# Last batch of top-32 attention with a low-rank mixer: first heads and results turned by the vector engine

## The chip, the cores and the metric

The kernel runs on one core of a Trainium2 chip. The metric is device time in microseconds (us) for one execution of the whole program. In the profile PE is TensorE (PEld its weight loads), DVE VectorE, ACT ScalarE, POOL GpSimd, and SP the engine whose queue issues the transfers.

## The reference

For each of 8 batches and 8 heads, attention over 576 positions of 64 values keeps the 32 largest scores of each row. The result, heads side by side, goes through a low-rank mixing along the sequence and a two-layer block. All is float32.

```python
scores = scale * np.matmul(q, k.transpose(0, 1, 3, 2))
kth = np.partition(scores, -32, axis=-1)[..., -32:-31]
scores = np.where(scores >= kth, scores, -1e9)
attn = np.exp(scores - scores.max(-1, keepdims=True))
attn = attn / (attn.sum(-1, keepdims=True) + 1e-09)
x = heads_side_by_side(np.matmul(attn, v))         # (8, 576, 512)
u = x + (x.transpose(0, 2, 1) @ U @ V).transpose(0, 2, 1)   # rank 32
out = u + np.maximum(u @ w_ch1, 0.0) @ w_ch2       # 512 -> 2048 -> 512
```

## The kernel before

*Tiling.* Two heads make a pair g; 4 pairs make a batch, 32 pairs the whole (`NPAIR`, `NP`). The 576 rows of a pair go in five chunks t: four of 128 rows for each of the two heads, and t=4 with the last 64 rows of both heads side by side. So there are 160 steps n = 5 g + t (`CH` is 5).

*One step of the main loop.* It works on several chunks at once. `front(n)` finds the 32nd largest score on DVE: MAX8 `first` (L385), then three times MATCH_REPLACE8 (L395) and MAX8 `m` (L399), for each of two heads; in t=4 there is one such chain, not two. ACT and POOL then mask the row and take the exponential into E (L402, L403, L419 to L421, L351). `scores(n+1)` (L320, L333) are on PE, copied to Ssb by ACT (L344 to L346); the next `first` waits for them. `turns(n-1)` turns E with PE transposes into PT (L474 and a copy on ACT, L475; the last 64 columns L479, L480). `values(n-2)` multiplies PT with v into O (L508, L512; L498 for t=4). PE's order in a step is: turns of the chunk two steps back, values of it, scores of the next chunk, with the block's matmuls in between.

*Second heads.* From step 30 on (`ROUNDED`), the second head (h=1) of the chunks t<4 isn't turned on PE (`shared`). `blocks(n-1)`, called in the middle of step n, lets DVE transpose its 32x32 blocks into y (L446). Four transfers write y to a buffer `away` in DRAM (L452), and one brings it back into the second half of PT (L456).

*The two-layer block as filler.* When the four pairs of a batch are mixed (`mixed`, L533 to L566), `mlp(b)` is put into `fillers`. `fill()`, called eight times in a step, adds a credit and draws so many matmuls of the block (L581 up into hT, L600 down), which spreads the block of batch b over the attention of batch b+1. The last batch's block has nothing to lie beside and comes at the end. The hT tiles are a ring of `HT` = 10 tiles of two blocks of rows; a half of a block (`SPAN`) uses 8 of them.

*Results.* A finished tile oT (L615, L616) is laid in `late`; `turned_back` turns it some matmuls later with two or three PE transposes (L648) and copies on ACT (L650, L652), and stores it with one or two transfers (L654, L659). In the last batch, all but the last tile are turned by DVE (L630) and stored by 8 or 12 transfers (L635, L640).

*Order.* PE, ACT, DVE and POOL each run their instructions in the order in which the code emits them; only SP's queue is ordered by the framework.

Of the kernel before, what the change touches and what calls it, by code (L numbers as in the profile page):

```python
# [8 lines left out]
F32 = mybir.dt.float32  # L9
# [17 lines left out]
def kernel(  # L27
# [29 lines left out]
    B, H, S, D = q.shape  # L57
    P = 128
# [3 lines left out]
    NF, NC = F // P, C // P  # L62
    NT, TAIL = 4, 64
    MAIN = NT * P
    HALF = S // 2
    assert S == MAIN + TAIL and D == 64 and H % 2 == 0 and C == 512 and TOPK % 8 == 0
    NPAIR = H // 2
    NP = B * NPAIR

    CH = NT + 1  # L70
# [3 lines left out]
    NV = 3  # L74

    BLK = 32
    HT = 10
    PE, ACT = mybir.EngineType.PE, mybir.EngineType.Activation
    DVE, POOL = mybir.EngineType.DVE, mybir.EngineType.Pool

# [2 lines left out]
    attn = ctx.enter_context(tc.tile_pool(name="attn", bufs=2))  # L83
# [11 lines left out]
    SPAN = ((0, 2 * P + TAIL), (2 * P + TAIL, S))  # L95
# [30 lines left out]
    def rows(t):  # L126
        return P if t < NT else TAIL

    def cols(t):
        return slice(t * P, t * P + rows(t))  # L130
# [4 lines left out]
    def half(h):  # L135
        return slice(h * D, (h + 1) * D)
# [98 lines left out]
    probs, PTs = {}, {}  # L235
# [198 lines left out]
    def shared(g, t):  # L434


        return t < NT and g * CH + t >= ROUNDED

    def blocks(g, t):


        E2 = probs[g, t]
        PT = attn.tile([P, 2 * NT + 1, P], F32, tag="PT", name="PT")
        PTs[g, t] = PT
        y = attn.tile([P, 4, NT, BLK], F32, tag="y", name="y", bufs=1)
        nc.vector.transpose(  # L446
            y.rearrange("p r c j -> p c r j"),
            E2[:, S + TAIL : 2 * S].rearrange("p (c r j) -> p c r j", c=NT, r=4),
        )
        away = dram.tile([P, 4, P], F32, tag="away", name="away")  # L450
        for a in range(4):
            nc.sync.dma_start(  # L452
                away[:, a].rearrange("(r i) n -> i r n", r=4),
                y[a * BLK : (a + 1) * BLK].rearrange("i r c j -> i r (c j)"),
            )
        nc.sync.dma_start(  # L456
            PT[:, NT : 2 * NT].rearrange("p a n -> p (a n)"), away.rearrange("p a n -> p (a n)")
        )

    def turns(g, t):  # L460


        E2 = probs.pop((g, t))
        nh = 2 if t < NT else 1
        if shared(g, t):
            PT = PTs[g, t]
        else:
            PT = attn.tile([P, 2 * NT + 1, P], F32, tag="PT", name="PT")
            PTs[g, t] = PT
        for h in range(1 if shared(g, t) else nh):  # L470
            tp = ps_t.tile([P, NT, P], F32, tag="tp", name="tp")
            for j in range(NT):
                a = h * (S + TAIL) + j * P
                nc.tensor.transpose(tp[:, j, :], E2[:, a : a + P], ident)  # L474
            nc.scalar.copy(PT[:, NT * h : NT * h + NT], tp)  # L475
            yield
        tp = ps_t.tile([P, P], F32, tag="tp", name="tp")
        a = MAIN if nh == 2 else S - P
        nc.tensor.transpose(tp, E2[:, a : a + P], ident)  # L479
        nc.scalar.copy(PT[:, NT * nh], tp)  # L480
        yield

    def inverse(g, lo, hi):
        den = dens[g][:, lo:hi]
        if g == NPAIR - 1:
            nc.vector.tensor_scalar_add(den, den, 1e-9)
        nc.vector.reciprocal(den, den)

    def values(g, t):

        PT = PTs.pop((g, t))
        va, vd, vt = (a[g % NV] for a in (vas, vds, vts))
        O = ps_t.tile([P, P], F32, tag="tp", name="O")
        if t == NT:
            den, x = dens[g], xs[g % 2]
            inverse(g, 2 * NT if g == NPAIR - 1 else 0, 2 * NT + 1)
            for j in range(NT + 1):
                nc.tensor.matmul(  # L498
                    O,
                    lhsT=PT[:, j],  # L500
                    rhs=va[:, :, j, :] if j < NT else vt,
                    start=(j == 0),
                    stop=(j == NT),
                )
            for h in range(2):
                nc.scalar.mul(x[half(h), NT, half(h)], O[half(h), half(h)], den[half(h), 2 * NT :])
            return
        nc.tensor.matmul(O, lhsT=vd, rhs=PT[:, 2 * NT], start=True, stop=False)  # L508
        PB = PT[:, NT : 2 * NT].rearrange("p a (c j) -> p c a j", c=NT) if shared(g, t) else None
        for j in range(NT):  # L510
            for h in range(2):
                nc.tensor.matmul(  # L512
                    O[half(h)],
                    lhsT=va[:, h, j, :],
                    rhs=PB[:, j] if h and shared(g, t) else PT[:, NT * h + j],
                    start=False,
                    stop=(j == NT - 1),
                )
        if t == 0:
            XTs[g] = attn.tile([P, MAIN], F32, tag="XT", name="XT")  # L520
        nc.scalar.copy(XTs[g][:, cols(t)], O)  # L521
# [49 lines left out]
    def mlp(b):  # L571
# [3 lines left out]
        for chunks, (lo, hi) in zip(PARTS, SPAN):  # L575
            w = hi - lo
            hTs = []
            for f in range(NF):
# [11 lines left out]
                if f % 2 == 0:  # L590
                    hT = mlpp.tile([P, 2, WIDE], F32, tag="hT", name="hT", bufs=HT)
                    hTs += [hT[:, 0], hT[:, 1]]
# [28 lines left out]
    def turned_back(b, chunks, lo, c, oT):  # L621


        def run():
            cs = slice(c * P, (c + 1) * P)
            if b == B - 1 and (lo, c) != (SPAN[1][0], NC - 1):

                w = sum(rows(t) for t in chunks)
                ob = mlpp.tile([P, 3 * P], F32, tag="ob", name="ob", bufs=2)
                nc.vector.transpose(ob[:, 0:w], oT[:, 0:w])  # L630
                for a in range(4):
                    cs = slice(c * P + a * BLK, c * P + (a + 1) * BLK)
                    ba = ob[a * BLK : (a + 1) * BLK]
                    for t in chunks[0:2]:
                        nc.sync.dma_start(  # L635
                            out[b, 0:MAIN, cs].rearrange("(m i t) c -> t i m c", i=BLK, t=NT)[t],
                            ba[:, OFF[t] - lo : OFF[t] - lo + P].rearrange("i (m c) -> i m c", c=BLK),
                        )
                    if NT in chunks:
                        nc.sync.dma_start(  # L640
                            out[b, MAIN:S, cs].rearrange("(m i) c -> i m c", i=BLK),
                            ba[:, 2 * P : 2 * P + TAIL].rearrange("i (m c) -> i m c", c=BLK),
                        )
                return
            tp = ps_t.tile([P, 3, P], F32, tag="tp", name="tp")
            for i, t in enumerate(chunks):
                n = rows(t)
                nc.tensor.transpose(tp[0:n, i, :], oT[:, OFF[t] - lo : OFF[t] - lo + n], ident)  # L648
            ob = mlpp.tile([P, 3, P], F32, tag="ob", name="ob", bufs=2)
            nc.scalar.copy(ob[:, 0:2], tp[:, 0:2, :])  # L650
            if NT in chunks:
                nc.scalar.copy(ob[0:TAIL, 2], tp[0:TAIL, 2, :])  # L652
            t = chunks[0]
            nc.sync.dma_start(  # L654
                out[b, 0:MAIN, cs].rearrange("(p t) c -> p t c", t=NT)[:, t : t + 2, :],
                ob[:, 0:2],
            )
            if NT in chunks:
                nc.sync.dma_start(out[b, MAIN:S, cs], ob[0:TAIL, 2])  # L659

        return run
# [4 lines left out]
    STEPS = NP * CH  # L666
# [6 lines left out]
    def fill(k=1):  # L673


        nonlocal due
        for _ in range(k):
            if passes:
                passes.pop(0)()
            if mixing and next(mixing[0], True):  # L680
                mixing.pop(0)
            due += share * (SHORT if t == NT else 1) * (EARLY if n <= 2 * ALONE + 2 else 1)
            while due > 0:
                if not fillers:
                    due = 0.0
                    break
                done = next(fillers[0], None)
                if done is None:
                    fillers.pop(0)
                else:  # L690
                    due -= done
# [3 lines left out]
    t = 0  # L695
# [5 lines left out]
    for n in range(STEPS + 2):  # L701
        g, t = divmod(n, CH)
# [8 lines left out]
        if n >= ALONE - 1 and n <= ALONE:  # L711

            if n < ALONE:
                next(last)
                values(*divmod(n - 3, CH))
                list(turning)
                next(here)
                next(last)
                scores(*divmod(n + 1, CH))
                values(*divmod(n - 2, CH))  # L720
# [51 lines left out]
        away = n <= STEPS and shared(*divmod(n - 1, CH))  # L772
# [26 lines left out]
        if n <= STEPS:  # L799
            turning = turns(*divmod(n - 1, CH))  # L800
# [3 lines left out]
        if t in (1, 3):  # L804
            next_params(1)
        next(here, None)
        fill()
    while mixing or fillers:
        fill()
# [31 lines left out]
```

## Time and profile before

| | |
|---|---|
| time, median of 3 runs | 1774.49 us (1774.05 to 1775.44) |
| profiled execution, span | 1773.6 us |
| DVE transpose y, L446 | 104 x 0.69 us |
| transfers away<-y, L452 | 416 of 64 KB, 1.8 us to landing |
| transfers PT<-away, L456 | 104 of 256 KB, 2.8 us to landing |
| PE transposes of E, L474 | 736, listed with 0.283 us each |
| PT copy on ACT, L475 | 184 x 0.585 us |

A row of the groups gives line, engine, operation, `out<-in`, the number of instructions and their mean duration. Matmuls overlap one another, and their ends in the profile are modelled, so what one of them costs is read from the distance of the starts.

### The profile page before, as it was taken

The numbers are of one execution on the slowest core, as the hardware profiler recorded it, in microseconds if no ns is written. First come the engines' busy times: TensorE is split into PE (matmuls) and PEld (weight loads), VectorE is DVE, ScalarE is ACT, GpSimd is POOL, SyncE is SP. The second block draws the span as 40 slices with busy tenths as digits, with TensorE's granted clock in tenths as the row PEclk, the third lists the DMA queues.
The fourth block names the chain that finished last, engine by engine and source line by source line (L and its number), as shares of the span: only waits on it lengthen the run. The fifth ranks groups of instructions, "written<-read, shape, count | busy, mean of one in ns | idle before, by whom it ended". The sixth has DMA issues, their size and how long they took to land.

```text
span 1773.6 us, 28992 instructions
## 1 busy us (share of the span) xinstructions
PE 1669.3 (94%) x9851; PEld 1257.5 (71%) x9851; DVE 1560.3 (88%) x3106; ACT 1029.4 (58%) x2682; POOL 846.8 (48%) x591
## 2 busy tenths in 40 slices
PE   4666789999999999999999999999999999999999
PEld 2434556677777877788777877788777877788677
DVE  7999989899999999999999999999999999994000
ACT  4778777555656656565656656565656656564100
POOL 4777677535354554545445454444445444453000
PEclk7687799999999999999999999999999999999999
DMA  3222332222223332222233232232233232211010
GB/s 95 88 82 73 88 85 61 50 59 71 58 67 80 66 72 56 67 68 64 64 71 79 62 70 62 65 70 63 63 73 80 59 73 60 53 50 45 4 15 13
DMA packets 275829, 112.79 MB, mean 64 GB/s; under 512 B 173920, under 2 KB 260192, under 8 KB 275680
## 3 DMA queue, kind: packets, MB, share of 16 engines
q1 hardware_dynamic: 274624, 110.68, 26.4%
q8 instruction: 77, 1.26, 0.3%
q14 instruction: 72, 0.59, 0.1%
q10 hardware_dynamic: 1056, 0.26, 0.1%
HBM read 74.15 MB, written 36.70 MB: 63 GB/s over the span
## 4 chain that ended last, share of the span: by engine, by line
PE 75%; DVE 16%; POOL 4%; ACT 3%; issue 2%; DMA 1%; SPq 0%; POOLq 0%; DVEq 0%
PE mm L581 25%; PE mm L600 24%; DVE rr L395 7%; PE sc L333 6%; PE O L512 6%; DVE m L399 6%; PE tp L474 3%; DVE first L385 2%; PE sc L320 2%; PE O L498 2%; PE up L556 1%; PE O L508 1%; POOL E L402 1%; PE up L558 1%; PE tp L648 1%
## 5 line engine op out<-in xcount | busy, mean ns | idle before, releaser
L399 DVE MAX8 m<-rr 128x8 f32<-128x576 f32 x864 | 614.7, 748 | 5.5
L600 PE MATMUL mm<-hT,w 128*128 128x256 f32 (+1 forms) x2048 | 547.4, 410 | 0.0
L581 PE MATMUL mm<-uT,w 128*128 128x256 f32 (+1 forms) x2048 | 541.5, 410 | 0.9 <-ACT hT L593 0.9
L402 POOL TENSOR_SCALAR E<-Ssb,m 128x576 f32<-128x576 f32 x127 | 281.1, 2214 | 411.7 <-DVE m L399 409.1
L581 PEld LDWEIGHTS mm<-uT,w 128*128 128x128 f32 x2048 | 371.7, 190 | 115.1 <-issue 26.0
L600 PEld LDWEIGHTS mm<-hT,w 128*128 128x128 f32 x2048 | 368.3, 190 | 106.8 <-issue 22.5
L395 DVE MATCH_REPLACE8 rr<-m,rr 128x576 f32<-128x576 f32 x576 | 427.2, 742 | 0.0
L421 POOL TENSOR_TENSOR Ssb<-Ssb,E 128x576 f32<-128x576 f32 x159 | 225.4, 1418 | 122.3 <-ACT E L420 121.7
L351 ACT ACTIVATE E<-Ssb,nmax 128x576 f32<-128x576 f32 x288 | 223.3, 776 | 52.4 <-POOL Ssb L403 34.9
L593 ACT ACTIVATE hT<-mm 128x320 f32<-128x320 f32 (+1 forms) x256 | 105.1, 411 | 240.4 <-PE mm L581 240.1
L385 DVE MAX8 first<-Ssb 128x8 f32<-128x576 f32 x288 | 203.3, 742 | 31.4 <-ACT Ssb L346 31.4
L395 DVE MATCH_REPLACE8 rr<-first,Ssb 128x576 f32<-128x576 f32 x288 | 211.8, 742 | 0.0
L403 POOL TENSOR_TENSOR Ssb<-Ssb,E 128x576 f32<-128x576 f32 x127 | 179.3, 1412 | 10.6
L333 PE MATMUL sc<-qkT 64*128 64x288 f32 x1024 | 170.6, 454 | 6.7 <-ACT Ssb L344 5.8
L474 PE MATMUL tp<-ident,E 128*128 128x128 f32 x736 | 116.0, 283 | 37.1 <-ACT XT L521 14.6
L512 PE MATMUL O<-PT,va 128*64 128x128 f32 x2048 | 146.3, 284 | 1.9 <-DMA PT<-away 1.9
L474 PEld LDWEIGHTS tp<-ident,E 128*128 128x128 f32 x736 | 92.1, 145 | 68.7 <-ACT XT L521 16.6
L475 ACT COPY PT<-tp 128x512 f32<-128x512 f32 x184 | 106.6, 585 | 49.0 <-PE tp L474 46.4
L512 PEld LDWEIGHTS O<-PT,va 128*64 128x64 f32 x2048 | 113.7, 140 | 19.0 <-DMA PT<-away 2.9
L420 ACT ACTIVATE E<-Ssb,least 128x576 f32<-128x576 f32 x159 | 123.3, 776 | 5.2
L333 PEld LDWEIGHTS sc<-qkT 64*128 64x128 f32 x1024 | 93.3, 198 | 45.3 <-issue 14.3
L613 DVE TENSOR_TENSOR oT<-uT,mm 128x320 f32<-128x320 f32 (+1 forms) x8 | 3.6, 455 | 137.1 <-PE mm L600 137.1
(81 smaller groups left out, 1574.0 us busy)
## 6 DMA issues: line engine op xcount, KB each, us to landing
away<-y SPq DMA_DIRECT2D x416, 64.0 KB, 1.8
PT<-away SPq DMA_DIRECT2D x104, 256.0 KB, 2.8
raw<-in_moe_w_ch_dram SPq DMA_DIRECT2D x32, 512.0 KB, 3.8
va<-in_v_dram SPq DMA_DIRECT2D x64, 128.0 KB, 2.3
out_dram<-ob SPq DMA_DIRECT2D x57, 128.0 KB, 2.2
ld<-in_q_dram SPq DMA_DIRECT2D x108, 64.0 KB, 2.4
ld<-in_k_dram SPq DMA_DIRECT2D x108, 64.0 KB, 2.4
ld<-in_q_dram SPq DMA_DIRECT2D x108, 8.0 KB, 2.2
```

The costliest lines, as they stand in the source:

```text
L333: nc.tensor.matmul(sc[:, h, 0:HALF], lhsT=qkT[half(h), 0, cols(t)], rhs=qkT[half(h), 1, i * HALF : (i + 1) * HALF], start=True, stop=True,)
L351: nc.scalar.activation(E, chunk, AF.Exp, bias=nmax, scale=SCALE, accum_out=total)
L385: nc.vector.max(ms[c], curs[c])
L395: nc.vector.match_replace(nxt, ms[c], curs[c], NEG)
L399: nc.vector.max(ms[c], curs[c])
L402: nc.gpsimd.tensor_scalar(Es[c], chunks[c], ms[c][:, 7:8], NEG, ALU.is_lt, ALU.mult)
L403: nc.gpsimd.tensor_tensor(chunks[c], chunks[c], Es[c], ALU.add)
L421: nc.gpsimd.tensor_tensor(chunks[c], chunks[c], Es[c], ALU.subtract)
L474: nc.tensor.transpose(tp[:, j, :], E2[:, a : a + P], ident)
L512: nc.tensor.matmul(O[half(h)], lhsT=va[:, h, j, :], rhs=PB[:, j] if h and shared(g, t) else PT[:, NT * h + j], start=False, stop=(j == NT ...
L581: nc.tensor.matmul(ph[:, 0:w], lhsT=w1[:, cc, f * P : (f + 1) * P], rhs=uT[:, cc, lo:hi], start=(cc == 0), stop=(cc == NC - 1),)
L600: nc.tensor.matmul(po[:, 0:w], lhsT=w2[:, f, c * P : (c + 1) * P], rhs=hTs[f][:, 0:w], start=(f == 0), stop=(f == NF - 1),)
```

## The change

It concerns the last batch and the result of the batch in front of it.

- `both` names the chunks t<4 of the pairs 28, 29 and 30, the first three of the last batch. Their first heads, too, are turned by DVE and transfers: `blocks` gets the head h as an argument and is called a second time, for h=0, at the end of the step, after DVE's last MAX8 in it. `turns` leaves these heads out, and `values` reads both halves of PT in the order of the blocks.
- y gets two buffers instead of one, and HT goes from 10 to 9 to make room.
- The results of batch 6 are turned back as those of batch 7 are: DVE in place of PE and ACT, 8 or 12 transfers in place of 1 or 2.

It is meant to take work from TensorE where the profile shows it full.

```diff
-    HT = 10
+    HT = 9
...
+    def both(g, t):
+        return t < NT and (B - 1) * NPAIR <= g < NP - 1
+
-    def blocks(g, t):
+    def blocks(g, t, h=1):
         E2 = probs[g, t]
-        PT = attn.tile([P, 2 * NT + 1, P], F32, tag="PT", name="PT")
-        PTs[g, t] = PT
-        y = attn.tile([P, 4, NT, BLK], F32, tag="y", name="y", bufs=1)
+        if h:
+            PTs[g, t] = attn.tile([P, 2 * NT + 1, P], F32, tag="PT", name="PT")
+        PT = PTs[g, t]
+        y = attn.tile([P, 4, NT, BLK], F32, tag="y", name="y")
         nc.vector.transpose(
             y.rearrange("p r c j -> p c r j"),
-            E2[:, S + TAIL : 2 * S].rearrange("p (c r j) -> p c r j", c=NT, r=4),
+            E2[:, h * (S + TAIL) : h * (S + TAIL) + MAIN].rearrange("p (c r j) -> p c r j", c=NT, r=4),
         )
...
-            PT[:, NT : 2 * NT].rearrange("p a n -> p (a n)"), away.rearrange("p a n -> p (a n)")
+            PT[:, NT * h : NT * h + NT].rearrange("p a n -> p (a n)"), away.rearrange("p a n -> p (a n)")
...
-        for h in range(1 if shared(g, t) else nh):
+        for h in range(0 if both(g, t) else 1 if shared(g, t) else nh):
...
-            if b == B - 1 and (lo, c) != (SPAN[1][0], NC - 1):
+            if b >= B - 2 and (b, lo, c) != (B - 1, SPAN[1][0], NC - 1):
...
         next(here, None)
+        if n <= STEPS and both(*divmod(n - 1, CH)):
+            blocks(*divmod(n - 1, CH), 0)
         fill()
```

More of the change, by code (lines that the diff above doesn't have):

```diff
@@ L508, in values @@
         nc.tensor.matmul(O, lhsT=vd, rhs=PT[:, 2 * NT], start=True, stop=False)
-        PB = PT[:, NT : 2 * NT].rearrange("p a (c j) -> p c a j", c=NT) if shared(g, t) else None
+        swapped = both(g, t), shared(g, t)
         for j in range(NT):
@@ L514, in values @@
                     lhsT=va[:, h, j, :],
-                    rhs=PB[:, j] if h and shared(g, t) else PT[:, NT * h + j],
+                    rhs=(
+                        PT[:, NT * h : NT * h + NT].rearrange("p a (c j) -> p c a j", c=NT)[:, j]
+                        if swapped[h]
+                        else PT[:, NT * h + j]
+                    ),
                     start=False,
```

## The prediction

> **What bounds the kernel now.** I read the page first: the busy shares and the 40 slices.
>
> ```profile
> PE 1669.3 (94%) x9851; PEld 1257.5 (71%) x9851; DVE 1560.3 (88%) x3106; ACT 1029.4 (58%) x2682; POOL 846.8 (48%) x591
> PE   4666789999999999999999999999999999999999
> DVE  7999989899999999999999999999999999994000
> ```
>
> Both PE and DVE show nines to slice 36; the last 3.5 slices are PE alone, the second block's multiplication of the last batch. The change sits just ahead of that, so I cut the end of the run with the table by windows. Its edges are the first MAX8 of pairs 28, 29, 30 and 31 (the last batch), the end of DVE's last MAX8, and the first matmul of the last MLP. Columns: span, then busy PE, PEld, DVE, ACT, POOL.
>
> ```profile
> 1418.98:1469.76 50.78, 50.66 (x314) 39.42 (x313) 48.52 (x97) 29.96 (x81) 24.60 (x17) 1.00 0.32 74
> 1469.76:1519.37 49.61, 49.61 (x288) 35.43 (x287) 48.51 (x97) 30.41 (x81) 23.27 (x15) 1.00 0.26 60
> 1519.37:1569.28 49.91, 49.91 (x300) 36.81 (x299) 48.52 (x97) 29.10 (x80) 24.94 (x17) 1.00 0.20 53
> 1569.28:1618.30 49.02, 49.02 (x314) 40.65 (x313) 47.36 (x95) 29.35 (x81) 23.15 (x15) 1.00 0.18 46
> 1618.30:1645.03 26.73, 25.41 (x154) 21.61 (x153) 0.22 (x1) 8.48 (x22) 4.63 (x5) 1.00 0.12 31
> 1645.03:1773.60 128.57, 124.77 (x516) 97.30 (x514) 7.02 (x15) 13.89 (x34) 0.00 (x0) 0.99 0.07 11
> ```
>
> The reader should see that PE is full and yet DVE has only 1.1 to 2.3 us to spare in a pair of 50. The waits of DVE, from 1418 to 1620 us, tell how much of that is real slack:
>
> ```profile
> DVE first L385 <- ACT Ssb L346: 3.3, 5, 1.0
> DVE y L446 <- ACT E L351: 1.4, 2, 0.7
> ```
>
> These are 4.7 us in all (some 4.1 of them from 1418.98 on, by the single waits), almost all in the step t=4 and at its end. The rest of DVE's idle is the bubble between dependent operations of the single chain of t=4; another operation cannot fill it.
>
> **What the Trainium skill says.** "VectorE: DVE Perf Modes", section "The three transpose paths": DVE transposes 32x32 blocks only, where TensorE does a whole 128x128. The trace agrees: each y of L446 is followed by four transfers to DRAM and one back, which put the blocks in place. "DMA: Bandwidth & Descriptors", "Anatomy of one DMA": about 2 us of a transfer are fixed, mostly the wait until its completion is known (said of the other issue path; for this one the trace has 1.8 us for the 64 KB transfers and 2.7 us for the 256 KB one). "Perfetto Trace Analysis", "Tensor Engine Instruction": a matmul's end is computed, not seen. It agrees: L474 has a mean of 283 ns, but from a block's first transpose to the next instruction it is 0.43 us for four (1513.27 to 1513.71), so I price by starts.
>
> **Part by part.**
>
> (1) *TensorE transposes of first heads removed.* 3 pairs x 4 steps x 0.43 us = 5.2 us of PE, and 12 copies of 0.585 us on ACT, which is no bound.
>
> (2) *Twelve more DVE transposes.* Duration 0.69 us; the next operation starts after 0.62:
>
> ```profile
> 1408.37 0.69 DVE L446 STREAM_TRANSPOSE y<-E 128x512 f32<-128x512 f32 x1
> 1408.99 0.05 DVE L395 MATCH_VALUE_LOAD rr<-m,rr 128x8 f32 x1
> ```
>
> With the extra bubble I take 0.63: 2.5 us per pair. That alone makes 48.5 + 2.5 = 51.0 us of DVE in a pair that lasts 49.6 to 50.8. DVE becomes the bound, and PE waits.
>
> (3) *Twelve more round trips through DRAM.* The new y stands after the last MAX8 of step n, just ahead of first(n+1), and its PT is wanted by O(n-1) in step n+1; behind that O stand scores(n+2) on the same engine, and first(n+2) waits for those. A quiet round trip by the trace: y at 1558.58, PT<-away issued 1562.49, landing 2.7 us later, 6.7 us from y's start. So with F the time of first in step n+1, PT lands at F - 0.63 + 6.7 = F + 6.1; O takes 1.03, and from the scores' start to first it is 2.1 us (1467.68 to 1469.76; 2.6 at 1516.78, where ACT is occupied). The next first can come at F + 9.2 to 9.7. Steps t=1 to 3 last 10.5 us or more and will last 11.1, so it is hidden there. Step t=4 has one chain, not two:
>
> ```profile
> 1512.46 0.74 DVE L385 MAX8 first<-Ssb 128x8 f32<-128x576 f32 x1
> 1515.75 1.09 PE L512 MATMUL O<-PT,va 128*64 128x128 f32 x16
> 1516.78 1.24 PE L333 MATMUL sc<-qkT 64*128 64x288 f32 x8
> 1519.37 1.42 DVE L385 MAX8 first<-Ssb 128x8 f32<-128x576 f32 x2 [0.46 <-ACT Ssb L346]
> ```
>
> There O ran 3.3 us after first; it will have to wait to about 6.1. The three t=4 steps, from first to first (1461.68, 1512.46 and 1562.08 to 1469.76, 1519.37 and 1569.28), last 8.08, 6.91 and 7.20 us now and become 9.2 to 9.7: together +5.4 to +6.9, say +6.0. The y of t=3 falls into the idle time so opened and costs nothing. The other nine y cost 9 x 0.63 = 5.7.
>
> (4) *Results of batch 6 turned back by DVE.* By following the credits of the fillers in the code (the trace confirms the places: L648 at 1523.98 directly ahead of O at 1524.31), the first four fall into pair 30, the other four after DVE's last MAX8. Each takes 0.51 us (L630, 128x320), 0.47 net; their oT is there 2 us or more before DVE gets to them (oT at 1517.96, DVE at 1520.7), so no wait. Three count 1.4 us; the fourth lies in the idle time of t=4. On PE this removes 4 x 0.33 and 4 x 0.22 us and the wait of 1.32 us at 1644.76, 3.5 us in all, of which 2.0 lie after the last O of the attention. Stores grow from 1 or 2 to 8 or 12 per result, 0.45 us of SP each.
>
> (5) *HT 10 to 9 and a second y.* One pair of hT stays free when a span starts; the second ACT write waits for a tile whose last reader is over 14 matmuls, some 3 us, back. Nothing.
>
> **The sum.** First of pair 31 comes 5.7 + 6.0 + 1.4 = 13.1 us late. Pair 31 itself adds no y; its two waits of 0.42 and 0.72 are regained in part: 12.7 at the first of its t=4. The end then hangs on this:
>
> ```profile
> 1616.08 0.71 DVE L446 STREAM_TRANSPOSE y<-E 128x512 f32<-128x512 f32 x1 [0.72 <-ACT E L351]
> 1616.82 1.77 SPq L452 DMA_DIRECT2D away<-y  x4
> 1621.10 0.34 SPq L456 DMA_DIRECT2D PT<-away  x1
> 1623.82 1.11 PE L512 MATMUL O<-PT,va 128*64 128x128 f32 x16
> 1644.76 0.44 PE L648 MATMUL tp<-ident,oT 128*128 128x128 f32 x2 [1.32 <-POOL oT L616]
> ```
>
> The last y could start at 1615.4 after its own chain, its PT then land 6.7 later at 1622.1, against O at 1623.82: slack of 1.7. O is thus 11.0 late; behind it PE has 20 us of fixed work, 2.0 less than before. The last MLP starts 9.0 late, and its 128.6 us do not change: 1774.5 + 9.0 = 1783.5 us.
>
> **The rivals.**
>
> *A, the forecast:* DVE is the bound, plus the round trip in t=4: 1783.5.
>
> *B, the round trip is hidden:* a transfer is faster, or its place in SP's queue better. Then a t=4 step is DVE's own 6.4 (1512.46 to the end of its last MAX8 at 1518.90) + 0.63; with 42.7 us for t=0 to 3 (1418.98 to 1461.68) the pairs become 42.7 + 6.4 + 2.5 = 51.6 us against 50.78, 49.61 and 49.91: +4.5, with the four results +6.4; minus 0.4, 1.7 and 2.0: +2.3, 1776.8. For it: only DVE's durations are certain. Against it: of the round trips here the quickest took 3.9 us from y to the last issue, and the quickest landing 2.5: 6.4 us.
>
> *C, SP crowded:* twelve stores (5.4 us of issue) stand ahead of a round trip in pair 30, eight (3.6 us) ahead of the last PT, as L654 stood ahead of it at 1620.5, and loads of 0.6 us each in pairs 28 and 29. About 5 us more: 1788.5. Against it: steps other than t=4 have 2 us to spare.
>
> *D, PE stays the bound:* PE is 100% busy and loses 5.2 + 3.5 = 8.7 us: 1765.8, the other side. For it: the chain of waits is 75% PE. Against it: DVE's busy time would have to pass the length of the pair; it could only hold if DVE's operations overlapped more than they do now.
>
> **How the numbers follow.** A 0.60, B 0.20, C 0.10, D 0.10. D leaves the range; B and C lie in it; with 2 us for unknown landings at either end: 1772 to 1791. All of A and C and a part of B are slower by over 0.2% (over 1778.0): 0.76; most of B within 0.2%: 0.15; D: 0.09.
>
> **What would show it.** DVE busy about 51 us in pairs 28 to 30, with PE falling to about 48 of 53 us and idle ahead of O L512, released by PT<-away; in t=4 first L385 waiting 2 us or more for Ssb; first of pair 31 near 1582; the last MLP's first matmul near 1654 and 128.6 us from there to the end. It is wrong if PE stays full in these windows (D), if the t=4 steps stay near 7 us (B), or if DVE waits at L630, which I cost at nothing.

## The result, and the profile after

| | before | after |
|---|---|---|
| time, median | 1774.65 us (1774.05 to 1775.44) | 1806.13 us (1804.24 to 1806.76) |
| ratio | | 1.0175 [1.0158, 1.0193] |
| profiled execution, span | 1773.6 us | 1802.5 us |

The change makes the kernel 31.5 us slower, where the forecast had 9. The page after, its busy shares and PE's row of slices:

```profile
PE 1676.2 (93%) x9783; PEld 1260.6 (70%) x9783; DVE 1570.4 (87%) x3126; ACT 1018.1 (56%) x2658; POOL 846.7 (47%) x591
...
PE   4666889999999999999999999999999988889999
```

PE has 68 instructions fewer and yet 6.9 us more of busy time, and slices 33 to 36 show eights: it waits there, and some of its work runs slower (shown further down). The table by windows, cut as before (first of pairs 28, 29, 30 and 31; then the last MLP; span, PE, PEld, DVE, ACT, POOL, clock, DMA share, GB/s):

```profile
1416.82:1476.71 59.89, 52.27 (x301) 39.47 (x300) 51.02 (x101) 28.05 (x77) 24.61 (x17) 0.94 0.38 95
1476.71:1535.66 58.95, 51.59 (x272) 35.96 (x271) 50.91 (x100) 28.53 (x77) 23.31 (x15) 0.91 0.38 91
1535.66:1600.73 65.07, 52.04 (x277) 37.48 (x276) 52.49 (x105) 25.38 (x70) 24.94 (x17) 0.87 0.31 72
...
1673.86:1802.50 128.64, 124.76 (x515) 97.39 (x513) 7.46 (x16) 13.86 (x34) 0.72 (x1) 0.99 0.07 11
```

The loss is all in three windows: 183.9 us instead of 150.3, so +33.6. From the first of pair 31 to the last MLP it is 73.1 us instead of 75.8 (-2.6), the last MLP is unchanged, and pair 28 happens to begin 2.2 us earlier. These four add up to the 28.9 us between the spans; the medians are 31.5 apart, since the profiled execution of the kernel after was the fastest of its four. DVE works as much as was foreseen, 51 us (52.5 in pair 30, with the results), but no longer bounds: these are 51 to 52.5 us of 59 to 65. The waits between 1400 and 1680 us (total, times, longest) say who does:

```profile
PE O L518 <- DMA PT<-away: 28.0, 9, 8.0
...
DVE first L385 <- ACT Ssb L346: 25.9, 7, 7.2
DVE ob L640 <- POOL oT L626: 24.4, 3, 10.5
```

(The prediction named a wait of DVE at the turning of the results, L630 there and L640 here, as a sign of being wrong. The wait is there, 24.4 us, but after DVE's last MAX8, where nothing hangs on it: e1 below has the same 24.4 us and is faster than the kernel before.) PE waits 28 us for data that come back from DRAM, and DVE nearly as long for the scores that stand behind that O on PE. Why the data are late is seen where the queue of SP (rows SPq) is laid beside DVE and PE. Chosen rows of the timeline around t=4 of pair 28:

```profile
1457.21 0.69 DVE L452 STREAM_TRANSPOSE y<-E 128x512 f32<-128x512 f32 x1
1458.19 4.51 SPq L458 DMA_DIRECT2D away<-y  x7
1460.71 0.70 DVE L452 STREAM_TRANSPOSE y<-E 128x512 f32<-128x512 f32 x1
1462.49 0.76 DVE L385 MAX8 first<-Ssb 128x8 f32<-128x576 f32 x1 [1.08 <-ACT Ssb L327]
1463.04 0.34 SPq L462 DMA_DIRECT2D PT<-away  x1
1463.42 0.42 SPq L458 DMA_DIRECT2D away<-y  x1
1463.90 0.59 SPq L245 DMA_DIRECT2D ld<-in_k_dram  x1
1468.42 0.71 DVE L452 STREAM_TRANSPOSE y<-E 128x512 f32<-128x512 f32 x1 [1.80 <-ACT E L351]
1469.16 0.30 SPq L458 DMA_DIRECT2D away<-y  x1
1469.63 0.34 SPq L462 DMA_DIRECT2D PT<-away  x1
1472.54 1.17 PE L518 MATMUL O<-PT,va 128*64 128x128 f32 x16 [3.60 <-DMA PT<-away]
1476.71 1.42 DVE L385 MAX8 first<-Ssb 128x8 f32<-128x576 f32 x2 [5.47 <-ACT Ssb L346]
```

The first head's y is made at 1460.71, and all four of its transfers to DRAM are issued by 1463.85 (three of them in the row x7, the fourth alone). Its PT<-away could follow 2 us later. But the framework has put one transfer of the *next* y in front of it; that y comes at 1468.42, SP stands still in between, and PT<-away is issued at 1469.63: 8.9 us after y, and 11.8 from y to O where the forecast counted 6.7. At t=4 of pairs 29 and 30 three and two transfers of the next y stand in front, and from y to O it is 9.6 and 9.2 us. In t=2 of pair 30 stores hold up the y's own transfers as well, until 1561.8: y at 1558.21, its PT<-away at 1567.93, O at 1570.75, 12.5 us. The t=4 steps last 14.2, 14.0 and 13.5 us (first at 1462.49, 1521.69, 1587.24 to the first of the next pair).

### The profile page after: what moved, and what is told of

Same layout as the page of the kernel before. It is cut to its first block, busy times and chain, and to the rows that moved or that the text cites. A ratio compares the mean times of both kernels' runs of the same rounds, so it can differ in the third digit from the quotient of the medians.

```text
span 1802.5 us, 29038 instructions
## 1 busy us (share of the span) xinstructions
PE 1676.2 (93%) x9783; PEld 1260.6 (70%) x9783; DVE 1570.4 (87%) x3126; ACT 1018.1 (56%) x2658; POOL 846.7 (47%) x591
## 4 chain that ended last, share of the span: by engine, by line
PE 73%; DVE 15%; POOL 4%; ACT 3%; DMA 3%; issue 1%; SPq 1%; DVEq 0%; POOLq 0%
PE mm L591 26%; PE mm L610 22%; PE sc L333 7%; DVE rr L395 6%; PE O L518 6%; DVE m L399 5%; PE tp L480 3%; DVE first L385 2%; PE sc L320 2%; PE O L504 1%; PE up L566 1%; DMA PT<-away 1%; PE O L514 1%; DMA away<-y 1%; POOL E L402 1%
## 5 line engine op out<-in xcount | busy, mean ns | idle before, releaser
L403 POOL TENSOR_TENSOR Ssb<-Ssb,E 128x576 f32<-128x576 f32 x127 | 179.1, 1410 | 10.6
L333 PE MATMUL sc<-qkT 64*128 64x288 f32 x1024 | 177.2, 468 | 6.4 <-ACT Ssb L344 5.3
L518 PE MATMUL O<-PT,va 128*64 128x128 f32 x2048 | 150.2, 290 | 29.9 <-DMA PT<-away 29.8
L480 PE MATMUL tp<-ident,E 128*128 128x128 f32 x688 | 108.1, 283 | 30.9 <-ACT x L512 11.3
L480 PEld LDWEIGHTS tp<-ident,E 128*128 128x128 f32 x688 | 85.4, 145 | 60.2 <-ACT XT L531 12.7
L481 ACT COPY PT<-tp 128x512 f32<-128x512 f32 x172 | 99.5, 584 | 48.2 <-PE tp L480 45.7
```

Of the source, the lines that this page charges most:

```text
L333: nc.tensor.matmul(sc[:, h, 0:HALF], lhsT=qkT[half(h), 0, cols(t)], rhs=qkT[half(h), 1, i * HALF : (i + 1) * HALF], start=True, stop=True,)
L403: nc.gpsimd.tensor_tensor(chunks[c], chunks[c], Es[c], ALU.add)
L518: nc.tensor.matmul(O[half(h)], lhsT=va[:, h, j, :], rhs=(PT[:, NT * h : NT * h + NT].rearrange("p a (c j) -> p c a j", c=NT)[:, j] if swap ...
```

## The experiments

Theory Q: the round trips cost more than forecast because of what stands ahead of PT<-away in SP's queue. Theory T: the round trips are too long in themselves, in any order (rival D in the expectation of e9 is the same). Theory S: the results do it, with their stores and with DVE's waits for them (rival R in the expectations of e1 and e2). The three pairs together (first of pair 28 to first of pair 31, from each profile) are the second measure; it leaves out where pair 28 begins, which varied by 4 us between profiles.

| run | time, us | ratio | three pairs, us |
|---|---|---|---|
| before | 1774.65 | | 150.3 |
| after | 1806.13 | 1.0175 [1.0158, 1.0193] | 183.9 |
| e1 results only | 1772.03 | 0.9983 [0.9976, 0.9990] | 151.1 |
| e2 heads only | 1803.76 | 1.0162 [1.0147, 1.0177] | 178.3 |
| e8 DVE's work only | 1777.23 | 1.0018 [1.0011, 1.0025] | 153.6 |
| e5 change, SP in the code's order | 1803.62 | 1.0168 [1.0152, 1.0183] | 174.5 |
| e7 change without t=2 | 1796.65 | 1.0131 [1.0112, 1.0150] | 168.7 |
| e9, e14, e17 heads only, clean queue | 1789.72, 1787.71, 1788.61 | 1.0082, 1.0068, 1.0072 | 169.0, 165.8, 162.8 |
| e11 change, clean queue | 1799.85 | 1.0146 [1.0132, 1.0159] | 170.6 |

**The parts alone.** e1 puts the new condition of the results into the kernel before, e2 the old one into the change:

```diff
-            if b == B - 1 and (lo, c) != (SPAN[1][0], NC - 1):
+            if b >= B - 2 and (b, lo, c) != (B - 1, SPAN[1][0], NC - 1):
```

> The kernel before with one part of the change alone: results of batch 6 turned back by DVE; no second heads, HT 10, one y. Theory Q (a transfer PT<-away stands in SP's queue behind the away<-y of a later y, which DVE has not written yet): there is one round trip per step, so the queue holds nothing back for long; 1771 to 1778 us. Rival R (the loss is made by the results: DVE waits for oT in the middle of its chain, and 8 or 12 stores block SP): 1782 us or more, with DVE waiting at its transpose of oT inside pair 30.

> The changed kernel with the results of batch 6 turned back by PE as before; HT 9 and two y as in the change. Theory Q: most of the loss stays, 1796 to 1806 us; only the store traffic of pair 30 is gone, and with it DVE's wait of 5.8 us in its t=2. Rival R: 1775 to 1788 us.

The results alone make the kernel 2.9 us *faster*. DVE's waits for them, 24.4 us, lie behind its last MAX8, and for scores it waits 2.1 us (before: 3.3):

```profile
DVE ob L630 <- POOL oT L616: 24.4, 3, 10.5
DVE first L385 <- ACT Ssb L346: 2.1, 3, 1.0
```

The heads alone are nearly the whole loss, 28.8 us; the results add 2.4 to that, with intervals that overlap. So theory S is not the cause of the loss. e12 turns only the last four results of batch 6 by DVE, those behind DVE's last MAX8:

```diff
+            if (b == B - 1 and (lo, c) != (SPAN[1][0], NC - 1)) or (b == B - 2 and lo):
```

> The kernel before with only the last four results of batch 6 turned back by DVE, those that come after DVE's last MAX8; nothing else. By the prediction's count for the part behind the last O of the attention, PE loses four times 0.22 us and a wait of 1.3 us: 1771.5 to 1773.5 us against about 1774.6. The rival (that part is not on the path that sets the end): 1774 to 1776 us.

1773.13 us, ratio 0.9989 [0.9982, 0.9995]: about 2 us less.

**DVE's twelve transposes alone.** e8 adds them to the kernel before, with HT 9 and two y buffers, into a tile that nobody reads:

```diff
+        y = attn.tile([P, 4, NT, BLK], F32, tag="y", name="y0")
+        nc.vector.transpose(
+            y.rearrange("p r c j -> p c r j"),
+            E2[:, 0:MAIN].rearrange("p (c r j) -> p c r j", c=NT, r=4),
+        )
```

> The kernel before with twelve transposes of first heads added on DVE, into a y that nobody reads; PE's transposes, the transfers and the results stay as before. It prices the DVE work alone. By the prediction's sums: +4.5 us at the first of pair 31, of which 0.4 are regained and 1.7 were slack: 1775.5 to 1778.5 us. If DVE's work is what the loss is made of, 1785 us or more.

Its windows, pairs 28 to 30:

```profile
1418.16:1469.40 51.24, 51.12 (x316) 39.80 (x315) 50.73 (x100) 30.50 (x82) 24.58 (x17) 1.00 0.31 72
1469.40:1520.60 51.20, 50.47 (x289) 35.59 (x289) 50.69 (x102) 30.19 (x80) 23.23 (x15) 1.00 0.26 60
1520.60:1571.80 51.20, 51.02 (x304) 37.42 (x303) 50.69 (x101) 28.50 (x79) 24.93 (x17) 1.00 0.20 52
```

Three equal pairs of 51.2 us around 50.7 of DVE, in which `first` never waits for scores: this is what a DVE bound looks like, though PE reads as nearly full, too. It costs 2.8 us in all and, with the buffers in it, leaves nothing for step (5).

**The order of the queue.** e3 (in the change) and e4 (in the kernel before) raise the priority of PT<-away:

```diff
+        with tc.high_priority():
             nc.sync.dma_start(
                 PT[:, NT * h : NT * h + NT].rearrange("p a n -> p (a n)"), away.rearrange("p a n -> p (a n)")
             )
```

> The changed kernel with PT<-away given high priority in the ordering of SP's queue; that queue then has four away<-y and their PT<-away together, for each y. Same instructions, same bytes. Theory Q: each round trip is back to about 6.7 us from the start of y, DVE waits 2 to 3 us at first of t=0 instead of 5.5 to 7.2, PE's matmuls after the wait run at full speed, and the time is what the prediction's own sum gives, 1782 to 1790 us. Rival T (the transfers themselves are slower because there are more of them): 1801 to 1807 us.

> The kernel before with the same high priority for PT<-away: the control for the order alone. Theory Q: with one round trip per step there is nothing to put right, 1772 to 1778 us. If the order of SP's queue as such is worth more, for instance by the loads that move with it, it is outside of that, and the comparison of the changed kernel has to be made against this one.

1805.67 and 1775.26: no effect. The trace of e3 has the seven away<-y ahead of PT<-away still, so the edit did not do what it was for, and the run says nothing on Q. e5 and e6 make SP keep the code's order in both kernels:

```diff
-    ctx.enter_context(tc.manual_schedule(engines={PE, ACT, DVE, POOL}))
+    ctx.enter_context(tc.manual_schedule(engines={PE, ACT, DVE, POOL, mybir.EngineType.SP}))
```

> The changed kernel with SP, too, in the order of the code; then every four away<-y are followed by their own PT<-away, and nothing of a later y stands between. The comparison is with the kernel before in the same order (e6). Theory Q: the twelve new round trips take 6.5 to 8 us each from the start of y; PE's waits for PT<-away fall from 28 us in all to 6 to 14; the time is 8 to 16 us above e6. Rival T (more transfers, each of them slower): the waits stay at 24 us or more and the time is 26 us or more above e6.

> The kernel before with SP in the order of the code, as the base for e5. Both theories: the last batch is as before (pairs of 49.5 to 51 us); the start of the program may change, by loads that no longer run ahead, so 1770 to 1800 us in all.

e6 is at 1774.55, as before, and e5 at 1803.62: by the numbers set down, this is T. But the trace shows that one obstacle had been exchanged for another. SP's queue in e5, and PE behind it:

```profile
1445.75 6.60 SPq L664 DMA_DIRECT2D out_dram<-ob  x2
1452.45 1.88 SPq L458 DMA_DIRECT2D away<-y  x4
...
1462.43 1.98 PE L518 MATMUL O<-PT,va 128*64 128x128 f32 x16 [4.50 <-DMA PT<-away]
...
1568.14 1.97 PE L518 MATMUL O<-PT,va 128*64 128x128 f32 x16 [10.92 <-DMA PT<-away]
```

In the code's order two stores sit in the queue from 1445.75 on, the second waiting for ACT's copy of its tile (1451.55), and the transfers of a y wait behind them; from 1556 to 1562 a block of twelve stores stands ahead of another y's. DVE's waits at the end of t=4 of pairs 28 and 29 fell to 0.7 and 2.9 us, while those of PE stayed at 27.9 in all. T has another measure against it: if the transfers were slower because there are more of them, they would land later, but between 1410 and 1610 us the medians from issue to landing are 1.8 us (away<-y) and 2.7 us (PT<-away) in the kernel before and in the changed one. e7 leaves out the new round trip of t=2, the one wanted in t=4:

```diff
-        return t < NT and (B - 1) * NPAIR <= g < NP - 1
+        return t < NT and t != 2 and (B - 1) * NPAIR <= g < NP - 1
```

> The changed kernel with the first heads of t=2 left to PE, so that no new round trip is wanted in the short step t=4; nine new y instead of twelve, framework's order of SP. Theory Q: in t=4 DVE had waited for 7.3, 7.2 and 6.3 us, before 1.7, 0.5 and 0.8; these waits go, those in t=2 and t=3 stay: 1783 to 1790 us. Rival (any new round trip costs about the same, wherever it is wanted): a quarter of the loss goes, 1796 to 1801 us.

1796.65, in the rival's range and not in Q's. The waits at the end of t=4 all but vanished (0.4, 0.4 and none), and with them 9.5 us of the loss; two others, behind stores, were 5.2 and 6.6 us long on PE (at 1565.89 and 1600.38). So the loss is not tied to t=4; other round trips are held up, too.

**A clean queue.** e9 has the heads only, the code's order, and the stores of the tiles that ACT copies are issued by ACT itself, so that SP never waits for ACT; e10 is the kernel before with the same two edits of the queues; e11 is the whole change with them, with the stores of batch 6 from ACT, too. The second edit:

```diff
-            nc.sync.dma_start(
+            nc.scalar.dma_start(
...
-                nc.sync.dma_start(out[b, MAIN:S, cs], ob[0:TAIL, 2])
+                nc.scalar.dma_start(out[b, MAIN:S, cs], ob[0:TAIL, 2])
```

> Heads alone (results of batch 6 by PE as before), SP in the order of the code, and the stores of results that ACT has copied issued from ACT, so that SP's queue holds loads, away<-y and PT<-away only, in the order in which DVE writes the y. Theory Q (the new round trips lose their time in SP's queue, behind transfers that wait for something later): pairs 28, 29 and 30 last 54 to 55 us each, as pair 29 did in e5, and the time is 8 to 15 us above e10. Rival D (a dependency of PE on the new transfers costs this much in any order): 22 us or more above e10.

> The kernel before with the same two edits of the queues, the base for e9 and e11. Both theories: 1772 to 1778 us.

> The whole change with the queues of e9; the 12 or 8 stores of each result of batch 6 are issued from ACT, too. Theory Q: pair 30, which lasted 65.1 us in the changed kernel and 64.1 in e5, comes to 55 to 58 us, and the time is within 4 us of e9. Rival S (the stores hurt wherever they are issued, by ACT's time or by traffic): 8 us or more above e9.

e10 is as before (1774.39). e9 takes 1789.72, 14.0 us less than the same heads in the framework's order (e2). It lies 15.3 us above e10, just past the 8 to 15 set down for Q and far from the 22 of D; its pairs of 54.7 to 57.8 us are longer than the 54 to 55 expected. So what stood ahead of the round trips was about half of the loss of e2, and not all of it; which of the two edits frees how much of it was not separated. Chosen rows of its t=4 in pair 28:

```profile
1459.83 0.69 DVE L452 STREAM_TRANSPOSE y<-E 128x512 f32<-128x512 f32 x1
1460.76 0.34 SPq L462 DMA_DIRECT2D PT<-away  x1
1461.20 1.82 SPq L458 DMA_DIRECT2D away<-y  x4
1464.86 0.34 SPq L462 DMA_DIRECT2D PT<-away  x1
1467.76 1.95 PE L518 MATMUL O<-PT,va 128*64 128x128 f32 x16 [3.43 <-DMA PT<-away]
```

Each PT<-away now stands directly behind its own four. From y to O it is still 7.9 us (7.1 and 8.0 in e14 and e17), not 6.7: the second head's PT<-away (1460.76) waits on SP for its own data and holds the next four up, and landing takes its 2.9 us.

e11 is 10 us slower than e9, where the same part of the change cost 2.4 with its stores on SP (after against e2). ACT is no free place for them. Waits of e11, and ACT in pair 30:

```profile
PE mm L591 <- ACT hT L603: 5.5, 2, 3.8
...
PE up L566 <- ACT Tb L562: 3.3, 1, 3.3
...
PE O L514 <- ACT PT L486: 2.9, 1, 2.9
```

```profile
1572.22 1.72 ACTq L645 DMA_DIRECT2D out_dram<-ob  x2
1573.98 0.44 ACTq L650 DMA_DIRECT2D out_dram<-ob  x1
1574.46 0.27 ACT L486 COPY PT<-tp 128x128 f32<-128x128 f32 x1 [8.11 <-DMA out_dram<-ob]
```

While ACT issues twelve stores it copies nothing, and PE waits for its copies: three waits of PE that the changed kernel itself does not have.

**The clock behind a gap.** In the change, where PE had waited long, the next instructions took nearly twice as long. PE of the changed kernel in t=4 of pair 29 (the last row is the O of pair 30), and the windows of the stretch in pair 29:

```profile
1530.68 1.98 PE L518 MATMUL O<-PT,va 128*64 128x128 f32 x16 [4.89 <-DMA PT<-away]
1532.59 2.29 PE L333 MATMUL sc<-qkT 64*128 64x288 f32 x8
...
1595.85 1.98 PE L518 MATMUL O<-PT,va 128*64 128x128 f32 x16 [5.07 <-DMA PT<-away]
```

```profile
1525.50:1530.60 5.10, 0.30 (x3) 0.10 (x1) 2.96 (x6) 1.19 (x3) 1.09 (x2) 0.75 0.50 124
1530.60:1534.90 4.30, 4.21 (x25) 2.85 (x25) 0.00 (x0) 0.90 (x2) 0.00 (x0) 0.50 0.55 124
1534.90:1540.00 5.10, 5.10 (x20) 3.63 (x21) 4.34 (x9) 3.01 (x9) 1.40 (x1) 1.00 0.41 93
```

The granted clock is 0.50 for 4.3 us behind the gap; O takes 1.98 instead of 1.09, the scores 2.29 instead of 1.24, and DVE waits for just these (0.00 busy). What this costs can be read in e9: from O to the next `first` at t=4 it is 4.7 us in pairs 28 and 30, where the clock had halved, and 3.1 in pair 29, where it had not (and 3.1 in all three of e17): 1.6 us each time. Theory K: a part of what is left in e9 is this clock. e13 fills three gaps of e9 with matmuls whose result is overwritten at once; e14 is e9 again, and e15 is e13 again beside it.

```diff
+        for _ in range({(0, 2): 18, (1, 1): 16, (2, 2): 10}.get((g - (B - 1) * NPAIR, t), 0)):
+            nc.tensor.matmul(O, lhsT=vd, rhs=vd, start=True, stop=True)
         nc.tensor.matmul(O, lhsT=vd, rhs=PT[:, 2 * NT], start=True, stop=False)
```

> e9_clean_heads with matmuls that compute nothing wanted (vd times vd into O, overwritten by the real ones that follow) put ahead of the O of three steps, where TensorE waits 3.43, 3.24 and 1.97 us for PT<-away and then runs O in 1.95, 1.98 and 1.85 us instead of 1.09: 18, 16 and 10 of them, some 2.1, 1.9 and 1.2 us, so that they fit into the waits and leave 1.3, 1.3 and 0.8 us of each. Theory K (a part of the loss is the slower clock after a gap): the three O take 1.09 again and the scores after them 1.24 instead of about 2.1; with some 4 us at half clock behind each gap, up to 2 us each come back: 3 to 6 us, 1783.5 to 1787 with the kernel before at 1774.5. Rival (the path is held by the round trip and by VectorE, so the slower clock is hidden behind other waits): the O take 1.09 but the time stays within 1.5 us of e9, 1788 to 1791, and the firsts at t=4 wait longer by what TensorE saves.

> The kernel of e9_clean_heads once more, on the same chip and beside the same runs of the kernel before as e15. 1787 to 1791, and in its profile 169 us from the first of pair 28 to the first of pair 31, as in e9.

> The kernel of e13_filled_gaps beside e14. In e13 the three pairs took 164.5 us in the profile instead of 169.0, but the medians of the two (1788.4 and 1789.7) and the ratios (1.0084 and 1.0082) did not differ by more than their intervals. Theory K (the slower clock behind a gap is a part of the loss): three pairs again near 164.5, and the time 3 to 5 us below e14. Rival (round trip alone): the pairs again differ by some us, and the time is within 1.5 us of e14.

1788.35, 1787.71 and 1787.92. In e13 and e15 the O behind the fillers take 1.09 again, and the time stays (three pairs: 164.5 and 164.9 us). But 18 fillers lasted 4.2 us, twice what was meant, and made O later than its data. e16 has 8, 8, 6 and 6 of them at four gaps, e17 is e9 a third time:

> As e13 and e15, with shorter fillers. There each filler ran as two instructions of 0.11 us, so that 18 of them took 4.0 us and not 2.1, and the O behind it came 0.6 to 1.3 us later than its data: the fillers may have eaten what the faster clock gave. Here 8, 8, 6 and 6 of them (1.8, 1.8, 1.3 and 1.3 us) stand ahead of the O of four steps whose gaps are 2.0 to 3.4 us in e9 and e14. Theory K (the slower clock behind a gap is a part of the loss): O 1.09 and scores 1.24 there, the three pairs 162 to 164.5 us instead of the 165.8 of e14, and the time 1.5 to 4 us below e17. Rival (the round trip alone): the pairs within 1 us of e17's, the time within 1 us.

> The kernel of e9 and e14 once more, beside e16: 1786 to 1791, the three pairs 165 to 169 us.

1788.62 and 1788.61: again no difference (three pairs of e16: 167.0 us). In e16 three of the four filled places ran at full clock; the clock halved at the fourth in spite of the filler (scores 2.25 after 1.50 us of filler and 2.96 of waiting), and behind two gaps that had none (2.75 and 1.76 us). So filling gains nothing that these runs can tell (each interval reaches some 2.5 us to either side). That the clock costs nothing does not follow: e9, e14 and e17 are one kernel, and where less of it ran at half clock the pairs were shorter. (Longer waits would make both, so this goes with the clock and does not prove it.) Windows of e9, then of e17:

```profile
1415.93:1472.44 56.51, 51.06 (x302) 39.44 (x301) 50.82 (x101) 28.39 (x78) 24.60 (x17) 0.97 0.43 101
1472.44:1527.17 54.73, 50.22 (x270) 34.99 (x269) 51.02 (x100) 28.17 (x77) 23.29 (x15) 0.94 0.38 86
1527.17:1584.97 57.80, 52.10 (x286) 37.45 (x285) 51.02 (x100) 26.97 (x76) 25.04 (x17) 0.94 0.44 107
```

```profile
1417.18:1472.13 54.95, 49.48 (x302) 38.26 (x301) 50.81 (x100) 28.28 (x78) 24.62 (x17) 1.00 0.40 97
1472.13:1525.75 53.62, 49.02 (x270) 34.43 (x269) 50.99 (x100) 28.08 (x77) 23.29 (x15) 0.97 0.38 95
1525.75:1580.02 54.27, 48.95 (x286) 35.59 (x285) 50.94 (x100) 26.66 (x76) 24.91 (x17) 1.00 0.46 105
```

169.0 against 162.8 us (e14, with 0.97 in all three: 165.8). DVE is busy for nearly the same time in both, 152.9 and 152.7 us.

## Why the prediction was wrong in size

The direction, the place and the last 128.6 us were right; step (3), the price of the round trips, was mis-sized, in two of its terms.

- *Step (1), and D.* PE lost the instructions, but none of it shows: PE is not the bound in these pairs. D is out. PE's busy time didn't fall to 48 us as forecast but rose to 52, because the work behind the gaps ran at half clock; in e17, nearly all at full clock, it is 49.0 to 49.5.
- *Step (2) held.* 51.0 us of DVE were forecast, 51.02 and 50.91 measured; by themselves the transposes cost 2.8 us (e8), since a DVE bound of 51.2 us (rival B's sum had 51.6) stands only 1 us above pairs of 50.
- *Step (3) is the one that failed.* Its first wrong term is the trip itself. "A quiet round trip by the trace: y at 1558.58, PT<-away issued 1562.49, landing 2.7 us later, 6.7 us from y's start" was taken from a queue that carried one such trip per step. In the changed kernel it is 11.8, 9.6 and 9.2 us in the three t=4 steps, because PT<-away stands in SP's queue behind transfers that themselves wait, for the next y or behind stores. So O starts 10.05, 8.99 and 8.61 us after `first`, where the forecast had 6.1: 9.4 us in all. Its second wrong term is what follows O: "O takes 1.03, and from the scores' start to first it is 2.1 us" (2.6 at most) was read at full clock. Behind these gaps it is 4.2, 5.0 and 4.9 us from O to the next `first`, not 3.1 to 3.6: 4.1 us in all. The prediction has no term for the clock. With both, the steps forecast at 9.2 to 9.7 us last 14.2, 14.0 and 13.5, which is 13.5 us above the 28.2 that three times 9.4 make. "So it is hidden there" failed once as well: the step t=2 of pair 30 lasts 16.9 us instead of 11.1. These 13.5 and 5.8 are 19.3 of the 20.5 us by which the three pairs pass the forecast (150.3 + 13.1 = 163.4).
- *In a clean queue the working of step (3) comes near.* The t=4 steps in e17, on DVE:

```profile
1461.69 0.72 DVE L385 MAX8 first<-Ssb 128x8 f32<-128x576 f32 x1
1472.13 1.42 DVE L385 MAX8 first<-Ssb 128x8 f32<-128x576 f32 x2 [3.63 <-ACT Ssb L346]
...
1516.69 0.76 DVE L385 MAX8 first<-Ssb 128x8 f32<-128x576 f32 x1
1525.75 1.42 DVE L385 MAX8 first<-Ssb 128x8 f32<-128x576 f32 x2 [1.79 <-ACT Ssb L346]
...
1570.61 0.72 DVE L385 MAX8 first<-Ssb 128x8 f32<-128x576 f32 x1
1580.02 1.42 DVE L385 MAX8 first<-Ssb 128x8 f32<-128x576 f32 x2 [2.61 <-ACT Ssb L346]
```

  They last 10.4, 9.1 and 9.4 us, and the three pairs 162.8, where the forecast for the heads alone makes 150.3 + 5.7 + 6.0 = 162.0. This is the quickest of the three profiles, with the fullest clock: the t=4 steps add up to 28.9 us in it, to 29.2 in e14 and to 32.3 in e9, where the forecast had 28.2.
- *Step (4) held in direction.* PE's gain is there: 2.9 us with all eight results (e1), 2 with the last four (e12). In the change it seems to be outweighed by the stores that stand ahead of the round trips: after is 2.4 us slower than e2, with intervals that overlap, and the step t=2 of pair 30 lasts 16.9 us in it against 12.3 in e2.
- *Step (5)*: nothing, within the 2.8 us of e8; it was not run alone.
- *Rival C* named the mechanism, and was sized as a time of issue (0.45 us a store, about +5). In these traces the entries ahead cost not only what they take to issue but also what they wait for: SP stood still for 4.7 us (1464.49 to 1469.16 above) in front of a single transfer.

The 31.5 us, then: 2.8 DVE's work; some 9 to 12 the round trips in a clean queue (e9, e14 and e17 lie 12 to 15 us above the kernel before), with the slower clock in it; 14 to 16 what stood ahead of them in SP's queue (e2 against these three; 9.3 to 15.5 by the three pairs), again with the clock behind the longer gaps in it; about 2 the results, which is within the noise. Open: how much of the loss is clock. At t=4 it is 4.1 us in the changed kernel, 3.2 in the profile of e9 and nothing in that of e17; the profiles of this one kernel differ by 6 us, and filled gaps gained nothing, so for the whole it is not measured. Also open is whether any order of one queue brings the whole change down to e17's figures, since e5 and e11 each exchanged one obstacle for another.

The best version found is e1, the results without the heads: 0.9983 [0.9976, 0.9990].

## What to carry to other kernels

A transfer that waits is priced by its place in its queue: list what is issued ahead of it, and for each entry what that waits for, before taking a round trip's length from a quiet stretch. More round trips per step change the queue that the quiet one was measured in, and an engine whose queue is ordered by the framework has to be looked at in the built kernel. Moving stores to a compute engine's queue moved their issue time onto that engine's work here.

## What was not expected of the hardware

- *Half clock behind a gap.* The Trainium skill, "TensorE: Matmul & The Clock Gate", section "Why this matters for your kernels", warns of gaps over some 3 us between matmuls, behind which TensorE runs at half rate. The traces agree in the rate (0.50) and show it for 4.3 us in the change. They differ in the bound: the clock halved after waits of 1.97 (e9) and 2.29 us (e14), and did not after 3.33 us in e17. On this path it hits the O and the scores that everybody waits for.
- *Issue on ACT.* Four times in e11 a dozen stores kept ACT from its copies, for 8.0, 6.7, 8.1 and 5.4 us; the forecast counted 5.4 us of SP for twelve. About 1 us of the 8.1 is a wait for DVE's transpose of the tile, so not all of it is issue.
